# Cutting the triangle of an inversion in four pieces on two engines, and re-dealing the weight conversion steps

## The chip, the core and the metric

The kernel runs on one core of a Trainium2 chip. The metric is the device time of one execution in microseconds (us). The engines that matter are PE (TensorE, matrix products), DVE (VectorE), ACT (ScalarE), POOL (GpSimd) and SP, which here only issues DMA transfers.

## The reference, cut to what matters

A recurrent attention block feeds a two-layer network. For each of 4 batches and 8 heads a 40 x 40 state is carried over 768 time steps:

```
for t in range(S):
    y[:, :, t] = einsum('bhd,bhde->bhe', r_t, state)
    Sa = einsum('bhde,bhe->bhd', state, a_t)
    state = state * w_t[:, :, None, :] - einsum('bhd,bhe->bhde', Sa, b_t) + einsum('bhd,bhe->bhde', v_t, k_t)
x = y.transpose(0, 2, 1, 3).reshape(3072, 320)
h = x @ w_in                      # 320 x 2048
out = (h * clip(h + 3, 0, 6) / 6) @ w_out   # 2048 x 320
```

The two weight matrices are 64-bit floats in memory and are converted to 32-bit floats on the chip, once per execution.

## The kernel before, in words

Time is cut into blocks of 64 steps. Two batches and one block make a unit; there are 24 units, and four consecutive units (NU = 4) make a group, so there are six groups. Within a block the recurrence is a triangular linear system. `prepare` builds for each unit the scaled operands and the matrix F of the system (stages W, gam, A, B, F, factor, K, E, EV). `invert` then inverts, for all 32 heads of a group at once, the triangular 32 x 32 blocks of F. `third_block` joins pairs of them with matrix products, and `step` runs the recurrence of a unit (stages RT, VT, R, C, S, U, UT, rS, sn, H, y, move, move2). The two-layer network of a unit is emitted in small pieces (`expand`, `contract`) between the stages of other units, so that PE always has something to do.

`invert` runs on DVE, with one part on POOL. It transposes F into the tile `fb` (L679). POOL then copies the part below the diagonal of `fb` into the tile `x` and writes zeros elsewhere with one `affine_select` of 1024 elements in each of 128 partitions (L682), and a small memset writes ones on the diagonal (L684). Thirty steps follow, i = 1 to 30, each of one product (`prod`, L691) and one addition into `x` (L697). Step i reads column i of `x` below row i and row i left of the diagonal, and updates columns 0 to i - 1. Two more transposes give `tb` and `tt` (L700, L705), which the matrix products of `third_block` read.

The order of work is written out by hand. `invert` is a generator in the deque `side`; `aside` advances it by one product or addition. The first inversion has little other work beside it: the loop `while not third` (L1180) advances it, and after every fifth advance it runs one early stage of the first two units. The later five inversions are advanced between pieces of the network.[...]

The weight conversion is a second generator, `load_weights`. The weights come in 20 pieces. A piece needs four DVE instructions and two on ACT: a mask (L316), then two ACT instructions on `parts` (L317, L319), two DVE instructions on the raw tile (L336, L340), and after that the product that writes the converted piece (L327). The raw tiles are reused, so a new load is issued on SP (L294) as old ones come free. One step of the generator is taken wherever a table says so:

- during the first inversion, at the advances numbered in `STEPS`;
- during the steps of the first four units, after the stages listed in `PLAN`: `2C:6` means that six conversion steps are taken at each pause of stage C of unit 2. `X` and `Y` are the two `third_block` parts.

PSUM tiles of the recurrence are taken in turn from a ring of five ("any"). A product that needs a slot waits until ACT or DVE has read the slot's former content.

## Time and profile before

| What | Value |
|---|---|
| time, median of 3 runs | 813.42 us (813.09 to 814.7) |
| the profiled execution | 812.7 us, of it 811.0 us span |
| PE busy | 737.0 us (91%) |
| DVE busy | 515.8 us (64%) |
| ACT busy | 319.8 us (39%) |
| POOL busy | 175.2 us (22%) |
| mean granted TensorE clock | 0.954 |
| `fb` transpose, each of 6 | 2.15 us |
| `affine_select`, each of 6 | 1.26 us |
| diagonal memset, each of 6 | 0.16 us |

The span goes from the first to the last instruction. Times of single instructions below are counted from the span's start. "Granted clock" is the share of full speed at which the throttle let PE run in a stretch. In the timelines a number in square brackets is the time that the engine sat idle before the instruction, and the name behind the arrow is the instruction that ended the idle time; "issue" there means that the profile shows no releaser.

### The profile page before, as it was taken

How to read it: one execution, taken by the hardware profiler on the slowest of the kernel's cores; microseconds unless marked ns; L12 is line 12 of the kernel's file. 1: busy time of each engine (PE TensorE's matmuls, PEld its weight loads, DVE VectorE, ACT ScalarE, POOL GpSimd, SP SyncE). 2: the span in 40 equal slices, each digit the busy share in tenths (PEclk: the TensorE clock that was granted, in tenths of full speed). 3: DMA queues.
4: the chain of work that ended last, by engine and by line, in shares of the span. 5: the costliest groups of instructions: out<-in, count | busy, mean ns of one | idle time of the engine just before them, and what ended most of it. 6: DMA issues, size and time to landing. Idle time of an engine off the chain costs nothing.

```text
span 811.0 us, 35829 instructions
## 1 busy us (share of the span) xinstructions
PE 737.0 (91%) x15832; PEld 625.2 (77%) x15832; DVE 515.8 (64%) x1188; ACT 319.8 (39%) x846; POOL 175.2 (22%) x301
## 2 busy tenths in 40 slices
PE   4634886989999989999999999999999999999998
PEld 3623775868778868888878888878888888888886
DVE  8878878769655689555698556698345784232210
ACT  2333753231545423645334553345453324322111
POOL 6403012420222130333122223124123102000000
PEclk9955787999999999999999999999999999999999
DMA  9592653420223330332231233222222101110000
GB/s 120 108 202 54 150 158 67 75 40 18 43 52 68 56 61 11 61 66 44 40 59 32 48 66 58 41 42 44 49 50 53 19 20 30 30 21 15 17 19 16
DMA packets 174218, 45.05 MB, mean 56 GB/s; under 512 B 157424, under 2 KB 172784, under 8 KB 174064
## 3 DMA queue, kind: packets, MB, share of 16 engines
q1 hardware_dynamic: 168672, 41.87, 27.1%
q8 instruction: 125, 2.05, 1.1%
q10 hardware_dynamic: 5392, 0.90, 0.7%
q14 instruction: 29, 0.24, 0.1%
HBM read 34.08 MB, written 3.93 MB: 47 GB/s over the span
## 4 chain that ended last, share of the span: by engine, by line
PE 75%; DVE 12%; DMA 4%; issue 4%; ACT 2%; SPq 2%; POOL 1%; ACTq 0%; DVEq 0%
PE h L1009 25%; PE o L1050 23%; PE any L474 4%; PE any L436 3%; PE any L924 3%; PE any L900 2%; PE any L446 2%; PE any L805 2%; DVE x L697 2%; DVE prod L691 2%; PE any L844 1%; PE any L865 1%; DVE wm L518 1%; PE any L648 1%; DMA R<-in_r_dram 1%
## 5 line engine op out<-in xcount | busy, mean ns | idle before, releaser
L1009 PE MATMUL h<-xt,win 128*128 128x128 f32 (+1 forms) x2304 | 250.2, 282 | 8.6 <-DVE gt L1025 6.8
L1009 PEld LDWEIGHTS h<-xt,win 128*128 128x128 f32 (+1 forms) x2304 | 230.4, 191 | 26.2 <-issue 10.3
L1050 PE MATMUL o<-wout,gt 128*128 128x320 f32 x768 | 232.5, 446 | 0.0
L1050 PEld LDWEIGHTS o<-wout,gt 128*128 128x128 f32 x768 | 139.6, 192 | 51.2 <-issue 1.6
L1025 DVE SCALAR_TENSOR_TENSOR gt<-gt,h 128x512 f32<-128x512 f32 x96 | 61.9, 681 | 67.1 <-ACT gt L1024 67.0
L1024 ACT ACTIVATE gt<-h,three 128x512 f32<-128x512 f32 x96 | 62.0, 685 | 97.8 <-PE h L1009 97.6
L939 POOL TENSOR_TENSOR yg<-ys,gam 128x512 f32<-128x512 f32 x22 | 39.0, 1772 | 162.6 <-DVE ys L937 100.8
L691 DVE TENSOR_TENSOR prod<-x 128x30 f32<-128x30 f32 (+9 forms) x180 | 62.8, 349 | 12.8 <-POOL x L682 7.3
L909 DVE TENSOR_TENSOR state<-any,state 40x160 f32<-40x160 f32 (+1 forms) x88 | 27.9, 321 | 66.7 <-PE any L900 40.1
L697 DVE TENSOR_TENSOR x<-x,prod 128x30 f32<-128x30 f32 (+9 forms) x180 | 65.4, 363 | 5.4
L621 POOL TENSOR_TENSOR KBt<-K,rgt 128x320 f32<-128x320 f32 x22 | 19.0, 866 | 222.0 <-ACT rgt L611 170.0
L483 DVE COPY_PREDICATED score<-mask,any 128x256 f32<-128x256 int32 x142 | 53.0, 436 | 6.0 <-PE any L474 5.5
L937 DVE TENSOR_TENSOR ys<-any,ys 128x256 f32<-128x256 f32 x44 | 16.6, 418 | 34.6 <-PE any L648 17.9
L654 ACT ACTIVATE EV<-any 64x160 f32<-64x160 f32 x88 | 23.9, 295 | 36.3 <-PE any L648 26.7
L518 DVE TENSOR_TENSOR_SCAN wm<-wm,start 128x528 f32<-128x528 f32 x24 | 37.6, 1567 | 0.8
L784 ACT ACTIVATE RT<-any 128x256 f32<-128x256 f32 (+1 forms) x44 | 15.5, 401 | 56.6 <-PE any L446 49.8
L507 DVE TENSOR_TENSOR_SCAN prods<-wm,start 128x528 f32<-128x528 f32 x24 | 30.0, 1256 | 10.6 <-ACT wm L504 10.6
L924 PE MATMUL any<-score,KBt 64*64 64x64 f32 x1536 | 31.9, 236 | 3.5 <-DVE state L909 3.5
L924 PEld LDWEIGHTS any<-score,KBt 64*64 64x64 f32 x1536 | 28.1, 148 | 6.1 <-DVE state L909 3.6
L759 ACT ACTIVATE tinv<-any 32x256 f32<-32x256 f32 x48 | 17.9, 374 | 30.1 <-PE any L749 24.7
L528 POOL COPY gam<-prods 128x256 f32<-128x256 f32 x24 | 22.5, 937 | 30.6 <-DVE prods L507 26.7
L1068 ACT ACTIVATE ob<-o 128x320 f32<-128x320 f32 x22 | 9.5, 434 | 46.3 <-PE o L1050 25.2
(197 smaller groups left out, 1077.7 us busy)
## 6 DMA issues: line engine op xcount, KB each, us to landing
V<-in_v_dram SPq DMA_DIRECT2D x96, 40.0 KB
out_dram<-ob SPq DMA_DIRECT2D x47, 80.0 KB
R<-in_r_dram SPq DMA_DIRECT2D x92, 40.0 KB
B<-in_b_dram SPq DMA_DIRECT2D x42, 80.0 KB
K<-in_k_dram SPq DMA_DIRECT2D x42, 80.0 KB
W<-in_w_dram SPq DMA_DIRECT2D x37, 80.0 KB
A<-in_a_dram SPq DMA_DIRECT2D x37, 80.0 KB
xt<-yg SPq DMA_DIRECT2D x72, 40.0 KB
```

Source lines behind the costliest of these rows:

```text
L474: nc.tensor.matmul(out=o[i][half(q), n, :], lhsT=lhs[half(i, D), n ^ (2 * q * swap), half(q)], rhs=rhs[half(i, D), n, half(q)], start=True ...
L483: nc.vector.copy_predicated(out=x[:, 4 * i:4 * i + 4, :], mask=mask4, data=o[i])
L507: nc.vector.tensor_tensor_scan(out=prods[:].rearrange("p r m i -> p (r m i)"), data0=wm[:, 0:SCAN], data1=start[:], initial=0.0, op0=ALU.m ...
L518: nc.vector.tensor_tensor_scan(out=back, data0=back, data1=start[:], initial=0.0, op0=ALU.mult, op1=ALU.add)
L691: nc.vector.tensor_tensor(out=pv, in0=_ap(x[:], (i + 1) * L + i, [[L, n], [0, i]]), in1=_ap(x[:], i * L, [[0, n], [1, i]]), op=ALU.mult,)
L697: nc.vector.tensor_tensor(out=rest, in0=rest, in1=pv, op=ALU.add)
L924: nc.tensor.matmul(out=y[q][half(s), pr, :], lhsT=o[name][half(q), h * D:h * D + SLOT], rhs=m[name][half(q), 4 * rs + 2 * s + j, :], start ...
L939: nc.gpsimd.tensor_tensor(out=yg[:], in0=m["ys"][:].rearrange("p r q t -> p r (q t)"), in1=o["G"][:], op=ALU.mult)
L1009: nc.tensor.matmul(out=hp[c][:, i, :], lhsT=lhsT, rhs=rhs, start=(begun[c] == 0), stop=(begun[c] == 3 * NQ - 1))
L1024: nc.scalar.activation(out=gt[:], in_=hp[c][:], func=AF.Relu, bias=three[:], scale=1.0)
L1025: nc.vector.scalar_tensor_tensor(out=gt[:], in0=gt[:], scalar=6.0, in1=hp[c][:], op0=ALU.min, op1=ALU.mult)
L1050: nc.tensor.matmul(out=op[:], lhsT=gts[c][:, n, :], rhs=wout[:, c * HJ + r * NQ + n, :], start=((split or r == 0) and c == 0 and n == 0), ...
```

## The change

`x` is now made in four quarters of 16 x 16. ACT copies the lower left quarter, which lies wholly below the diagonal. POOL selects the upper left quarter and writes its diagonal, then zeros the upper right quarter, selects the lower right one and writes its diagonal. The dependence tracking gives the first product of the steps a wait for the upper left selection and for ACT's copy only; the rest of POOL's work may run beside the steps. The first wait of a step for the lower right quarter's diagonal stands at the addition of step 4.

The second and third edits deal the conversion steps by other tables. On DVE they shift the position of conversion instructions by a few places between 40 us and 140 us; on ACT they shift the `parts` pairs with them. No instruction of PE or SP changes its place.

```diff
         x = inv.tile([P, L, L], F32, name="x", tag="x", bufs=1)
-        nc.gpsimd.affine_select(out=x[:], in_=fb[:], pattern=[[1, L], [-1, L]],
-                                compare_op=ALU.is_gt, fill=0.0, base=0, channel_multiplier=0)
-        nc.gpsimd.memset(_ap(x[:], 0, [[L + 1, L]]), 1.0)
+
+        def cut(rows, columns, first):
+            nc.gpsimd.affine_select(out=x[:, rows, columns], in_=fb[:, rows, columns], pattern=[[1, HL], [-1, HL]],
+                                    compare_op=ALU.is_gt, fill=0.0, base=0, channel_multiplier=0)
+            nc.gpsimd.memset(_ap(x[:], first * (L + 1), [[L + 1, HL]]), 1.0)
+
+        HL = L // 2
+        nc.scalar.activation(out=x[:, HL:, 0:HL], in_=fb[:, HL:, 0:HL], func=AF.Copy)
+        cut(slice(0, HL), slice(0, HL), 0)
+        nc.gpsimd.memset(x[:, 0:HL, HL:], 0.0)
+        cut(slice(HL, L), slice(HL, L), HL)
         for _ in range(3):
             yield
...
-    STEPS = (1, 6, 8, 9, 10, 14, 17, 25, 31, 36, 42, 48, 58, 61, 64)
+    STEPS = (2, 4, 9, 12, 13, 16, 20, 24, 26, 31, 39, 52, 59, 61, 64)
...
-    PLAN = """X X:2 0U:3 0UT 1R
-              0sn 0H:2 Y:2
-              1U:1 1UT:3 0y:4
-              2RT:2 Y
-              1sn 1H 2VT:2 0move 0move2
+    PLAN = """X:1 X:1 0U:3 0UT 1R
+              0sn:1 0H:2 Y:2
+              1U 1UT:3 0y:2
+              2RT:1 Y
+              1sn:1 1H:1 2VT:1 0move 0move2
               1y:3 2R
-              2S:3 3RT
-              1move 1move2 2U:1 2UT 2C:6
-              3R:3 3VT
+              2S:3 3RT:1
+              1move 1move2 2U:1 2UT 2C:7
+              3R:3 3VT:1
               2rS:3 2sn:3 2H:4 3S:2
-              2y:2 3U:3 3UT:7 3C:5
-              3rS:4 3sn 3H 2move
-              3y 2move2
+              2y:3 3U:2 3UT:7 3C:5
+              3rS:2 3sn:1 3H:2 2move
+              3y:2 2move2
```

## The prediction

> **What bounds the kernel now.** I read the page first (busy shares, granted clock), then the groups of the inversion's lines, then the table by stretches, then the timelines of DVE, POOL, ACT, PE and SP where PE stops.

> ```profile
> PE 737.0 (91%) x15832; PEld 625.2 (77%) x15832; DVE 515.8 (64%) x1188; ACT 319.8 (39%) x846; POOL 175.2 (22%) x301
> PE   4634886989999989999999999999999999999998
> PEclk9955787999999999999999999999999999999999
> ```

> PE is the bound. From about 140 us on it hardly stops; before that it waits for DVE, DMA and ACT. As its order and work stay, time is gained only where PE stands still or runs at a lower clock. Now the inversion:

> ```profile
> L682 POOL TENSOR_SCALAR_AFFINE_SELECT x<-fb x6: 1264/1264/1267, 29.3 to 633.5; 128x1024 f32<-128x1024 f32 x6
>   DVE prod L691: 7.3, 6
> ```

> DVE waits 7.3 us in all for POOL's selection: 0.39 us in the first group, 1.37 to 1.43 us in the other five. Whether that costs anything is told by the stretches (PE, PEld, DVE, ACT, POOL busy; clock; DMA) and, below the dots, by the timeline (start, duration, engine).

> ```profile
> 174.00:176.00 2.00, 1.98 (x43) 1.24 (x36) 1.10 (x3) 0.00 (x0) 1.94 (x5) 1.00 0.00 0
> 176.00:178.00 2.00, 0.00 (x0) 0.00 (x0) 1.93 (x3) 0.00 (x0) 2.00 (x4) 1.00 0.00 0
> 178.00:180.00 2.00, 0.81 (x24) 0.84 (x28) 1.83 (x7) 0.00 (x0) 0.35 (x1) 0.86 0.66 112
> 180.00:185.00 5.00, 5.00 (x69) 3.62 (x62) 3.63 (x12) 2.17 (x8) 0.00 (x0) 0.72 0.18 34
> ...
> 174.83 0.20 DVE L691 TENSOR_TENSOR prod<-x 128x30 f32<-128x30 f32 x1 [1.43 <-POOL x L682]
> 175.07 0.86 DVE L697 TENSOR_TENSOR x<-x,prod 128x30 f32<-128x30 f32 x1
> 178.66 0.76 DVE L483 COPY_PREDICATED score<-mask,any 128x256 f32<-128x256 int32 x2
> 174.99 0.87 POOL L621 TENSOR_TENSOR KBt<-K,rgt 128x320 f32<-128x320 f32 x1
> 179.19 1.36 PE L648 MATMUL any<-V,score 64*64 64x40 f32 x32 [3.21 <-issue]
> ```

> In the second inversion PE stands from 175.98 to 179.19. The profile names no releaser, but the product L648 reads the masked score, which DVE writes from 178.66 behind three step pairs: the inversion's late start is PE's wait. After it the clock falls: 1 us windows show 0.50 from 180 to 182, and the four L1050 products there take 2.43 us against 1.27.

> ```profile
> 394.18 2.15 DVE L679 STREAM_TRANSPOSE fb<-F 128x1024 f32<-128x1024 f32 x1 [4.65 <-ACT F L591]
> 397.71 0.21 DVE L691 TENSOR_TENSOR prod<-x 128x30 f32<-128x30 f32 x1 [1.37 <-POOL x L682]
> 415.17 1.13 PE L1009 MATMUL h<-xt,win 128*128 128x128 f32 x8 [1.26 <-DVE gt L1025]
> ```

> In the fourth inversion DVE has no further idle time from 397.71 to the gt at 414.42 for which PE waits 1.26 us. The fifth is a copy of it (PE waits 1.26 us at 531.94); the third waits 1.43 us at 293.00, again for gt. After the sixth (from 631.30) no PE wait is listed.

> ```profile
> 41.26 0.43 DVE L316 TENSOR_SCALAR parts<-tinv 128x512 uint32<-128x512 uint32 x1 [1.08 <-DMA tinv<-in_moe_w_in_dram]
> 58.29 0.78 DVE L483 COPY_PREDICATED score<-mask,any 128x256 f32<-128x256 int32 x2 [2.78 <-PE any L474]
> ```

> In the first inversion DVE waits at 41.26 for a weight load and at 58.29, by way of PE, for the load of R. What is won before these is waited away.

> **The new gate.** DVE's first product waits for the later of two. POOL's selection of 256 elements: by the row of 1024 (1.264 us), 0.32 us if time goes with elements, 1.26 if none of it does; POOL copies of 256 elements took 0.40, so I take 0.43. ACT's copy of 256 elements: the ACT copy of 320 elements within SBUF (L799) took 0.46, those of 256 from PSUM 0.37 to 0.40; I take 0.43. ACT was idle at the end of fb in inversions two to five, so the gate falls from 1.26 to 0.43: DVE starts 0.83 us earlier. POOL's five pieces sum to 0.43 + 0.15 + 0.30 (memset of 256, between rows of 0.25 for 192 and 0.16 for 32) + 0.43 + 0.15 = 1.46 us against 1.26 + 0.16: KBt, queued behind them, moves by 0.1 us.

> [...] The rows: the addition at 175.07 took 0.86 us beside POOL's KBt product, and 0.21 us in the fourth inversion without it, while the product at 30.59 took 0.20 us beside POOL's diagonal memset. [...] The second selection reads `fb` and now stands beside the steps; before, DVE idled through it. [...] I take 0.3. On ACT the copy waits for fb with all behind it: rgt (second inversion, to 174.6, needed at 175.1), RT (third, 0.4 us late, read only behind network pieces), gt (sixth: 631.29 becomes 633.9, but DVE takes it at 634.7 instead of 635.46).

> **The sum, against the profiled 812.7 us.**

> *27 to 72 us.* DVE's stream starts 0.39 us earlier and meets both waits above. `STEPS` puts the same 12 conversion instructions before the last transpose, and the same three behind the score of 58.29, so `tb` stays at 67.84. 0 us (0.5 better to 1 worse).

> *72 to 140 us.* At 76 to 80 DVE idles 3.52 us; `PLAN` moves one L340 (0.60) into it. The next parts pair on ACT ends 0.6 us earlier, so does zs behind it, for which PE's L865 waits 0.47 us at 83.56. PE's L749 then ends 0.4 us earlier than 88.23, which frees tile x for the load at 88.33. From there SP issues back to back until 116.58, and the last but two of its weight loads (115.45, landed 120.85) starts the DVE chain of conversions, score, scans and gt that ends with the state at 136.26, for which PE waits 3.51 us. That chain keeps its sum (L327, 0.6, moves from its end to its middle). So -0.4 us. ACT's S at 98.74 comes some 1.5 us earlier, but U now stands behind another pair and ends where it did: nothing.
> One step turns the other way: U of unit 3 (ACT, 117.99) now stands behind the parts pair of the load of 120.85, so at 122.8. The score product L474, which needs U's ring slot, moves from 118.05 to 123.1, and what follows it at half clock (1.2 + 0.95 + 1.1 + 0.95 + 1.0 us) ends L436 at 128.2 instead of 126.04. PE had 3.5 us to spare before 136.54, so this costs nothing, and leaves a shorter stop ahead of 136 us. After the stop the clock is at 0.50 until about 141.9, 2.7 us of PE work lost. I count 1.0 of these as saved. Together -1.4 us (from 1 worse to 3.1 better).

> *Second inversion.* fb ends at 173.41, the gate at 173.96; two pairs are through by 175.0, the third pair meets KBt (two of its instructions cost one POOL product each, 0.85), the score starts at 176.9 and PE at 177.4: 1.8 us less (1.0 if a fourth instruction is caught, 2.6 if only one). PE's stop is then 1.4 us. Does the clock fall? Rows: stops of 3.21, 2.89 and 2.61 us (from 176, 110.6 and 96.8) were each followed by some 3.4 us at 0.50, the stop of 1.43 us at 291.6 by none. [...] I go by the trace: 3.4 us x 0.5 = 1.7 us saved. Together -3.5 us (1.0 to 4.3).

> *Third to fifth.* DVE's chain to the gt shortens by 0.83 - 0.3 = 0.53 us, less than PE's waits of 1.43, 1.26 and 1.26: -1.6 us (0.9 to 2.5). What is late next is the same gt, by 0.7 us. *Sixth.* 0.

> Sum -6.5: 806.2 for an execution like the profiled one. That lay 0.7 below the median of 813.42, so the median goes to 806.9.

> **The rivals.**
> *Clock not saved (0.27).* The stop stays over 2 us, or the clock falls anyway; 72 to 140 gives 0.4. For it: the shortest stop seen before a fall is 2.61 us, so the limit may be just above 1.43. 0.4 + 1.8 + 1.6 = 3.8 less: 809.6.
> *The wait changes its name (0.10).* The selection is mostly fixed cost, or ACT's copy waits behind F and wakes late: the first product starts as before and the collision with the second selection eats the rest. For it: nothing shows a selection of 256. Against: POOL's times grow with elements (memsets: 0.16 for 32, 1.80 for 2048). 813.0.
> *Slower (0.08).* U of unit 3 behind the conversion pair, at 118 to 128 us. Each us that the load lands later holds U, the score, and both transposes of W; past PE's slack (3.5 less 2.1 used) it counts fully, and it decides the sign once it exceeds all else, when the load lands over 6 us after 120.85. Against: SP's order is unchanged, and this load took 5.4 us, the longest other 6.35. Then 816.

> **How the numbers follow.** The forecast has 0.55: 806.9, own range 804 to 809. The measurement can tell about 0.2%, 1.6 us. Faster (under 811.8) are the forecast, the first rival and 0.02 of the second: 0.84. Same 0.08 (the rest of the second), slower 0.08. The range, 803.9 to 812.0, takes in the better bounds of all terms in part and the first rival whole.

> **What would show it.** Right: the first product 0.5 us after fb instead of 1.3; PE's stop at 176 under 2 us and no 0.50 in the clock behind it; the waits for gt in inversions three to five near 0.7 us; `tb` of the first still some 9.5 us behind the score. Wrong: a selection of 256 near 1 us; steps of 0.6 us beside the second selection; PE stopped past 137 us for a score or transpose queued behind U.

## The result, and the profile after

The changed kernel took 808.35 us (median of 4 runs, 807.46 to 809.5) where the kernel before took 813.25 us beside it (4 runs, 812.76 to 814.7). The ratio is 0.9938, with a 95% interval of 0.9917 to 0.9958: 5 us or 0.6% faster. Measured again, they stood at 807.88 (12 runs) and 812.35 us (26 runs), ratio 0.995 (0.9931 to 0.9968). The forecast was 806.9.

The profiled execution took 807.46 us, of it 805.7 us span. Lines of the page that answer to those shown of before (busy time, then the span in 40 slices):

```profile
PE 737.2 (91%) x15832; PEld 625.7 (78%) x15832; DVE 516.3 (64%) x1188; ACT 322.5 (40%) x852; POOL 177.2 (22%) x319
PE   4734868999999989999999999999999999999998
PEclk7755788999999999999999999999999999999999
```

PE does the same work, 737 us, in a span that is 5.3 us shorter; ACT has six instructions more, POOL eighteen. The time was gained where PE stood still. The new pieces, by tile (min, median and max in ns), and who waited for the selection:

```profile
L684 POOL TENSOR_SCALAR_AFFINE_SELECT x<-fb x12: 505/506/508, 29.4 to 629.4; 128x256 f32<-128x256 f32 x12
L686 POOL MEMSET x<- x12: 126/128/130, 30.0 to 629.9; 128x16 f32 x12
L691 POOL MEMSET x<- x6: 312/312/313, 30.2 to 629.1; 128x256 f32 x6
L689 ACT ACTIVATE x<-fb x6: 416/417/417, 29.3 to 628.3; 128x256 f32<-128x256 f32 x6
  DVE prod L699: 3.1, 5
```

DVE waits 3.1 us for the selection in place of 7.3. The line numbers have moved: L684 is the selection (L682 before), L699 the product (L691), L705 the addition (L697), and what follows `invert` stands 8 lines lower. The second inversion, from the timeline (start, duration, engine, operation, in brackets the idle time before it):

```profile
169.85 0.51 POOL L684 TENSOR_SCALAR_AFFINE_SELECT x<-fb 128x256 f32<-128x256 f32 x1 [14.79 <-issue]
170.39 0.21 DVE L699 TENSOR_TENSOR prod<-x 128x30 f32<-128x30 f32 x1 [0.67 <-POOL x L684]
...
170.87 0.51 POOL L684 TENSOR_SCALAR_AFFINE_SELECT x<-fb 128x256 f32<-128x256 f32 x1
170.87 0.53 DVE L699 TENSOR_TENSOR prod<-x 128x58 f32<-128x58 f32 x1
...
171.56 0.86 POOL L621 TENSOR_TENSOR KBt<-K,rgt 128x320 f32<-128x320 f32 x1
...
171.70 0.82 DVE L699 TENSOR_TENSOR prod<-x 128x84 f32<-128x84 f32 x1
172.38 0.86 POOL L621 TENSOR_TENSOR KBt<-B,rgt 128x320 f32<-128x320 f32 x1
172.56 0.78 DVE L705 TENSOR_TENSOR x<-x,prod 128x84 f32<-128x84 f32 x1
...
173.26 0.76 DVE L483 COPY_PREDICATED score<-mask,any 128x256 f32<-128x256 int32 x2
...
173.79 0.89 PE L648 MATMUL any<-V,score 64*64 64x40 f32 x30 [1.49 <-issue]
```

Three things are to be seen. The gate, DVE's wait for the selection, is 0.67 us, 1.43 before. The second selection more than doubles the second product: 0.53 us, where the fourth inversion of before, with nothing on POOL beside it, has 0.22:

```profile
398.19 0.22 DVE L691 TENSOR_TENSOR prod<-x 128x58 f32<-128x58 f32 x1
```

And of the three step pairs ahead of the score only two instructions meet KBt and are long now (0.82, 0.78), where four had been (0.86, 0.79, 0.83, 0.81), as POOL starts KBt one and a half step pairs later in DVE's count. PE's stop falls from 3.21 to 1.49 us. The table of the stretches cut at 3.40 us (length; busy PE, PEld, DVE, ACT, POOL; granted clock; DMA share; GB/s) shows what follows:

```profile
171.40:174.80 3.40, 1.91 (x67) 1.54 (x66) 3.19 (x8) 0.03 (x1) 3.37 (x7) 0.99 0.02 2
174.80:178.20 3.40, 3.40 (x37) 2.07 (x37) 3.08 (x10) 1.06 (x4) 0.16 (x1) 0.51 0.59 99
```

The clock falls to half for 3.4 us all the same. In the fourth inversion the wait for gt goes from 1.26 to 0.83 us:

```profile
391.11 0.21 DVE L699 TENSOR_TENSOR prod<-x 128x30 f32<-128x30 f32 x1 [0.62 <-POOL x L684]
...
391.60 0.53 DVE L699 TENSOR_TENSOR prod<-x 128x58 f32<-128x58 f32 x1
...
408.89 1.13 PE L1017 MATMUL h<-xt,win 128*128 128x128 f32 x8 [0.83 <-DVE gt L1033]
```

Ahead of it, between the first and the second transpose:

```profile
56.75 0.77 DVE L483 COPY_PREDICATED score<-mask,any 128x256 f32<-128x256 int32 x2 [2.62 <-PE any L474]
117.41 0.43 DVE L316 TENSOR_SCALAR parts<-raw_fb 128x512 uint32<-128x512 uint32 x1 [0.99 <-DMA raw_fb<-in_moe_w_out_dram]
119.59 1.13 PE L474 MATMUL any<-RT,VT 40*64 40x64 f32 x30 [3.36 <-ACT U L857]
133.62 1.89 PE L932 MATMUL any<-score,KBt 64*64 64x64 f32 x62 [2.85 <-DVE state L917]
```

The score in the first of these lines (58.29 before) is called the first score below. All of them stand 1.5 to 3.4 us earlier than before, except L474, which waits 3.36 us for U behind the conversion pair and still ends with 2.85 us to spare.

Where the 5.3 us of the two spans lie is read from the six transposes `fb`, which start each inversion. From one to the next the two profiled executions took, before and after: 144.29 and 140.47; 110.86 and 108.73; 112.09 and 112.06; 116.78 and 117.62; 120.34 and 120.15 us. So -3.8 between the first and the second, -2.1 in the second, and in sum +0.6 over the third to fifth, where -1.6 had been forecast.

### The profile page after: what moved, and what is told of

It reads as the page before. It is cut to its first block, busy times and chain, and to the rows that moved or that the text cites. A ratio compares the mean times of both kernels' runs of the same rounds, so it can differ in the third digit from the quotient of the medians.

```text
span 805.7 us, 35863 instructions
## 1 busy us (share of the span) xinstructions
PE 737.2 (91%) x15832; PEld 625.7 (78%) x15832; DVE 516.3 (64%) x1188; ACT 322.5 (40%) x852; POOL 177.2 (22%) x319
## 3 DMA queue, kind: packets, MB, share of 16 engines
q8 instruction: 125, 2.05, 1.0%
## 4 chain that ended last, share of the span: by engine, by line
PE 72%; DVE 10%; issue 5%; DMA 4%; ACT 2%; SPq 1%; POOL 1%; ACTq 0%; DVEq 0%; POOLq 0%
PE h L1017 25%; PE o L1058 23%; PE any L474 4%; PE any L436 3%; PE any L932 3%; PE any L446 2%; PE any L908 2%; DVE prod L699 2%; PE any L813 2%; DVE x L705 2%; PE any L852 1%; DMA R<-in_r_dram 1%; PE any L648 1%; PE any L873 1%; PE any L757 1%
## 5 line engine op out<-in xcount | busy, mean ns | idle before, releaser
L699 DVE TENSOR_TENSOR prod<-x 128x30 f32<-128x30 f32 (+9 forms) x180 | 64.3, 357 | 8.6 <-POOL x L684 3.1
L705 DVE TENSOR_TENSOR x<-x,prod 128x30 f32<-128x30 f32 (+9 forms) x180 | 65.2, 362 | 5.4
L621 POOL TENSOR_TENSOR KBt<-K,rgt 128x320 f32<-128x320 f32 x22 | 19.1, 866 | 217.7 <-ACT rgt L611 214.1
L483 DVE COPY_PREDICATED score<-mask,any 128x256 f32<-128x256 int32 x142 | 53.0, 436 | 6.0 <-PE any L474 5.6
L528 POOL COPY gam<-prods 128x256 f32<-128x256 f32 x24 | 22.5, 938 | 29.9 <-DVE prods L507 26.0
```

What stands on the lines that cost most here:

```text
L483: nc.vector.copy_predicated(out=x[:, 4 * i:4 * i + 4, :], mask=mask4, data=o[i])
L699: nc.vector.tensor_tensor(out=pv, in0=_ap(x[:], (i + 1) * L + i, [[L, n], [0, i]]), in1=_ap(x[:], i * L, [[0, n], [1, i]]), op=ALU.mult,)
L705: nc.vector.tensor_tensor(out=rest, in0=rest, in1=pv, op=ALU.add)
```

## The experiments

My theory after the result: the gate (0.67 us for 1.43) and the DVE steps that are long beside POOL's products (two of about 0.8 us for four) make the second inversion's gain, the tables make that ahead of it, and the rest of the differences belongs to single executions. The rivals: the early first score is the change's own, the collision eats the gate, or the gain comes from one of the edits alone.

**The selection in quarters alone.** `invert` of the changed kernel, `STEPS` and `PLAN` of before.

```diff
-    STEPS = (2, 4, 9, 12, 13, 16, 20, 24, 26, 31, 39, 52, 59, 61, 64)
+    STEPS = (1, 6, 8, 9, 10, 14, 17, 25, 31, 36, 42, 48, 58, 61, 64)
...
-    PLAN = """X:1 X:1 0U:3 0UT 1R
+    PLAN = """X X:2 0U:3 0UT 1R
...
```

> The selection in quarters alone, with STEPS and PLAN as before. My theory (the inversion's gate and the tables gain in different places): inversions 2 to 5 as in the changed kernel (PE's stop ahead of the EV products in the second one 1.5 us in place of 3.2, waits for gt near 0.8 in place of 1.26), so the second inversion brings 2.1 us and the later ones little more; what the changed kernel had won before its second transpose (3.67 us) mostly stays away, because it hangs on the order of the tables. About 810.5 us, 2.2 faster than the kernel before. Rival A (the early 1.5 us at the first score belong to the earlier start of the steps): the score near 58.3 us comes at 56.8 here too, and the time is about 809. Rival B (the collision of the second selection with the second product, 0.31 us in each inversion, and KBt on GpSimd beside the third step eat the gate's gain): no change, 812.5 to 813.5.

809.25 us, ratio to before 0.9965 (0.9947 to 0.9984), some 3 us. First score at 57.34 (rival A had 56.8; before has 58.29), the second transpose at 170.90, and from there 108.85 us to the third. PE's waits in that stretch (us in total, times, longest):

```profile
PE any L648 <- issue: 1.5, 1, 1.5
```

The gate works alone as it does with the tables; rival B, no change, falls.

**The tables alone.**

```diff
+        nc.gpsimd.affine_select(out=x[:], in_=fb[:], pattern=[[1, L], [-1, L]],
+                                compare_op=ALU.is_gt, fill=0.0, base=0, channel_multiplier=0)
+        nc.gpsimd.memset(_ap(x[:], 0, [[L + 1, L]]), 1.0)
-        def cut(rows, columns, first):
...
```

> STEPS and PLAN of the changed kernel with the whole triangle selected by GpSimd as before. My theory: the stretch between the third blocks and the second inversion gains about 2 us (raw_x load about 0.3 earlier, raw_fb converted about 3 us earlier), the first score stays near 58 us or moves to 57, the second transpose comes 2 to 3.5 us sooner, and from there on every wait is that of before (PE's stop 3.2 us, waits for gt 1.26 to 1.43): 809.5 to 811. Rival A (the early 1.5 us belong to the earlier start of the steps): the second transpose comes only 2.1 us sooner, about 811. Rival B (the tables only fit the new steps' timing): no gain or a loss, 813 to 815.

810.95 us, ratio 0.9987 (0.9968 to 1.0006): about 1 us less, which the measurement cannot tell from nothing. First score at 55.71, earlier than expected and the earliest of all profiles, second transpose at 167.56 us, raw_fb converted at 118.28, then the waits of before:

```profile
PE any L648 <- issue: 3.2, 2, 3.1
```

**Both kernels once more, unchanged.**

> The changed kernel as it is, for a second profile. If what was won by the first score (58.3 to 56.8 us) and in the landing of raw_fb (5.4 to 4.4 us after its issue) belongs to the change, both stand here as before: score near 56.8, raw_fb converted near 117.4 us, time 807.5. If they belong to one execution only, the score comes between 57 and 58.5 or raw_fb a microsecond later, and the time is about 809.4, the other of the two values that the four runs took. PE's stop in the second inversion 1.5 us and the half clock after it for one or two windows of 3.4 us: in my theory the fall is a matter of how the stop lies to the windows and may be absent in this profile.

> The kernel before as it is, for a second profile. If the 1.5 us at the first score and the 1 us of raw_fb's landing are the change's: score at 58.3 us, R issued at 40.4 and raw_fb converted at 120.8 us again. If they vary from one execution to the next: one of them 1 us or more off. The clock after the three long stops of PE (2.6, 2.9 and 3.2 us) falls to half again.

| profile of | first score | raw_x load | raw_fb converted | second `fb` | third `fb` |
|---|---|---|---|---|---|
| before | 58.29 | 88.33 | 120.85 | 171.23 | 282.09 |
| before, again | 57.13 | 87.43 | 120.58 | 170.98 | 281.41 |
| after | 56.75 | 86.52 | 117.41 | 167.56 | 276.29 |
| after, again | 56.35 | 86.26 | 118.95 | 170.04 | 277.67 |

The repeat of before has its first score at 57.13 and its R issued at 39.57 in place of 40.37: with nothing changed it moves by 1.2 us. The repeat of after stays early, at 56.35. Of the 3.7 us by which the second transpose came early, 2.5 are gone in the repeat of after, although its raw_x load is as early. The second inversion's stop is 1.47 us again, and this time the clock does not fall (1.00 behind the stop), as my theory allowed: the stretch takes 107.63 us in place of 108.73.

**One table each.** PLAN of the changed kernel with the old `STEPS`, then `STEPS` with the old `PLAN`, quarters in both.

> The changed kernel with the STEPS table of before: quarters and PLAN only. My theory (the score of the first window comes between 56 and 58.4 us from one execution to the next, whatever STEPS says; PLAN's earlier third-block pieces bring raw_x, the conversion of raw_fb and so the second transpose forward): from the first score to the raw_x load 29.0 to 29.9 us as in the changed kernel (30.0 to 30.3 before), the second transpose near 169.5 us, 808.5 in all. Rival (STEPS brings it, by the order of the conversion pieces among the first steps): raw_x 30.1 us behind the score, second transpose near 171, 809.5 in all.

> The changed kernel with the PLAN of before: quarters and STEPS only. My theory: raw_x load 30.0 to 30.3 us behind the first score, second transpose near 171 us as in both profiles of the kernel before and with the quarters alone, 809.5 in all. Rival (STEPS brings the gain): second transpose near 169.5 us, 808.5.

808.33 us, ratio 0.9954 (0.9937 to 0.997), and 809.78 us, ratio 0.9967 (0.9949 to 0.9986): by time they can't be told apart. By the profiles, from the first score to the raw_x load 29.07 us with the new `PLAN` alone and 30.02 with the old, as my theory had it. The second transpose stands at 169.80 and 170.06, the latter between the two expectations. Over all profiles the stretch between the first and second transpose took 143.14 to 144.29 us in the four with the old `PLAN` (mean 143.8) and 140.47 to 143.53 in the ten with the new one (mean 142.3), those of the experiments below with them.

**KBt off GpSimd.** In the second group's last two units the two KBt products of each go to VectorE, behind the scores.

```diff
...
+            if NU + 2 <= i < 2 * NU:
+                o["late"] = rest
+            else:
+                rest(nc.gpsimd)
...
+            if "late" in o:
+                o.pop("late")(nc.vector)
...
```

Here `rest` holds the two products, and the second part stands in the stage EV, behind the scores.

> The changed kernel, with the four KBt products of the second group's last two units taken from GpSimd and given to VectorE behind the scores. My theory (while GpSimd multiplies two tensors, VectorE's steps stand still: 0.82, 0.78 and 0.75 us where such a step takes 0.22 to 0.27 alone): the third step's pair takes 0.5 us in place of 1.60, PE's stop ahead of the EV products falls from 1.49 to 0.4 us, and as the 3.41 us window with the stop is then busy to over 0.8, the clock doesn't fall after it. VectorE pays four products of 0.5 us and gets back about 1.6. In all 1.1 to 2 us less than the changed kernel, 806.5 where that one has 808. Rival (the long pairs are long for their own reasons, or the next wait ends just as late): the stop stays near 1.4 us, and the time is 808 to 809, by the added work on VectorE.

807.01 us, ratio 0.9931 (0.991 to 0.9951). From its timeline:

```profile
173.15 0.53 DVE L707 TENSOR_TENSOR prod<-x 128x58 f32<-128x58 f32 x1
...
173.96 0.25 DVE L707 TENSOR_TENSOR prod<-x 128x84 f32<-128x84 f32 x1
174.24 0.25 DVE L713 TENSOR_TENSOR x<-x,prod 128x84 f32<-128x84 f32 x1
174.41 0.76 DVE L483 COPY_PREDICATED score<-mask,any 128x256 f32<-128x256 int32 x2
...
174.94 0.40 PE L654 MATMUL any<-V,score 64*64 64x40 f32 x4 [0.35 <-issue]
```

The third pair takes 0.50 us in place of 1.60 and PE's stop goes to 0.35: that KBt on POOL held the steps up is shown. The clock holds (1.00 from 174.7 to 181.5 us). But the stretch takes 107.64 us, as in the repeat of after, whose clock also held: the 1.1 us of stop were given back. Two new waits of PE, 0.17 for the state and 0.26 for zs, stand near the third blocks, which need the end of the inversion, and that end came hardly sooner (tb 30.43 us behind the transpose, 30.56 in the repeat). The rival on the next wait holds for this part, and by time this run can't be told from the changed kernel.

**The second selection only written.** The lower right quarter is filled with zeros in place of being selected; its data are left out.

```diff
-        cut(slice(HL, L), slice(HL, L), HL)
+        nc.gpsimd.memset(x[:, HL:, HL:], 0.0)
+        nc.gpsimd.memset(_ap(x[:], HL * (L + 1), [[L + 1, HL]]), 1.0)
```

> The changed kernel with the second selection, that of the lower right quarter, replaced by a fill with zeros of the same 256 elements: that quarter's data are left out. My theory (an instruction of GpSimd that reads SBUF keeps the two-input product of VectorE waiting, one that only writes does not): the second product takes 0.22 us in place of 0.53 in each of the six inversions, PE's waits for gt in the third to fifth fall from 0.8 to 0.5 us. About 1 us less than the changed kernel in all, 0.3 in the profile at each. Rival (the product is slow because two engines write the same tile, or by its shape): 0.53 us stays and nothing moves.

```profile
172.34 0.31 POOL L692 MEMSET x<- 128x256 f32 x1
172.37 0.22 DVE L700 TENSOR_TENSOR prod<-x 128x58 f32<-128x58 f32 x1
...
PE h L1018 <- DVE gt L1034: 0.5, 1, 0.5
```

Same tile, same elements, but POOL only writes: the product is back at 0.22 us, and the wait for gt in the fourth inversion at 0.51 in place of 0.83. So the product is longer by 0.31 us beside a selection that reads `fb`, and not beside a fill that only writes, and the 0.31 us pass to PE in full (0.32). 807.63 us, ratio 0.9934 (0.9907 to 0.996); 1 us is too little for the time to show.

**The transpose in halves.** The first half brings the columns that the first selection and ACT's copy read, so these run beside the second half.

```diff
+        for part in (slice(0, L // 2), slice(L // 2, L)):
+            nc.vector.transpose(out=fb[:, :, part].rearrange("p t s -> p s t"),
+                                in_=F[:, :, part].rearrange("p h s -> p s h"))
-        nc.vector.transpose(out=fb[:].rearrange("p t s -> p s t"),
-                            in_=F[:, :, 0:L].rearrange("p h s -> p s h"))
```

> The changed kernel with the transpose ahead of the inversion in two halves, so that the first selection and ScalarE's copy run beside the second half. My theory (the gate is a bare wait, and a transpose with one input does not exclude GpSimd): VectorE's wait of 0.67 us for the first selection goes to 0.0 to 0.1 in inversions 2 to 6; the halves cost 0.05 to 0.1 us more together; the second selection now collides with the first step in place of the second, for 0.3 to 0.5 us. Net 0.3 to 0.6 us for each of inversions 2 to 5: PE's waits for gt 0.8 to about 0.4, the stop in the second inversion 1.49 to about 1.0 and no fall of the clock after it. 806 where the changed kernel has 808. Rival (the selection does collide with the transpose, or the step loses what the gate won): no change, 808.

```profile
170.02 2.22 DVE L680 STREAM_TRANSPOSE fb<-F 128x512 f32<-128x512 f32 x2 [0.39 <-ACT F L572]
...
171.33 0.50 POOL L685 TENSOR_SCALAR_AFFINE_SELECT x<-fb 128x256 f32<-128x256 f32 x1 [13.81 <-PE any L606]
...
172.13 0.17 DVE L700 TENSOR_TENSOR prod<-x 128x30 f32<-128x30 f32 x1
...
172.57 0.35 DVE L700 TENSOR_TENSOR prod<-x 128x58 f32<-128x58 f32 x1
...
175.31 0.54 PE L648 MATMUL any<-V,score 64*64 64x40 f32 x6 [0.30 <-issue]
```

804.73 us, ratio 0.9902 (0.9882 to 0.9921): 7.8 us below before, the lowest median of all. The first step has no wait, the first selection takes its 0.50 us beside the transpose, the second adds only 0.13 us to the second product (0.35), and PE's stop, expected at 1.0, is 0.30. PE's wait for gt in the fourth and fifth inversion is 0.26 us. In the third it stays at 0.93 (0.98), because the gate stays there:

```profile
278.29 0.87 POOL L621 TENSOR_TENSOR KBt<-B,rgt 128x320 f32<-128x320 f32 x1
279.12 0.50 POOL L685 TENSOR_SCALAR_AFFINE_SELECT x<-fb 128x256 f32<-128x256 f32 x1
279.66 0.21 DVE L700 TENSOR_TENSOR prod<-x 128x30 f32<-128x30 f32 x1 [0.50 <-POOL x L685]
```

The first half is there at 278.09, but POOL is busy with KBt until 279.1, when the second half ends too.

**KBt on VectorE and the transpose in halves together.**

> Both of the last: the transpose in halves, and the four KBt products on VectorE behind the scores. My theory: the two add up. PE's stop in the second inversion is gone (under 0.3 us), the clock holds, waits for gt in the later inversions 0.4 us: 805 to 805.5, the fastest of all. Rival: PE's next wait (for R, for gt) takes the place of the stop, and the time stays at 806.5 or above.

806.25 us, ratio 0.9911 (0.9889 to 0.9933). PE's stop is gone, yet the stretch takes 106.90 us against 106.88 with the halves alone. The two do not add up; the rival stands. By time it can't be told from the halves alone.

**V loaded later.** This asked for the stops at the score product L474 in the third to fifth inversion.

```diff
-            if i > 2 * NU:
-                fetch("V", i)
             for name in "BK":
...
             o["E"] = masked(x)
+            if i > 2 * NU:
+                fetch("V", i)
```

> The changed kernel with the load of V in the later groups (units past 2 NU) issued behind the scores' masking in place of behind KBt. It asks where the gain of the waits for gt in the third to fifth inversion went: in every profile PE stands still for 0 to 1.3 us at one score product some 64 to 71 us behind each transpose, about 1.9 us after the first V load's issue, with no wait that the profile shows. My theory (the V loads' traffic holds PE's own supply up): with V later these stops go from PE's list at that product, and come elsewhere at most in part; 1 to 2 us less than the changed kernel. Rival (the stop belongs to the place in PE's program, or to its own completion counts): it stays at that product, 0.6 to 1.3 us in two or three of the three groups, and the time is unchanged at 808.

> The same move of the V load on the kernel with the transpose in halves, the fastest so far. My theory: 803.5 to 804.5, the stops at the score product gone, waits for gt 0.26 in the fourth and fifth inversion. Rival: 804.7 as with the halves alone, the stops still there; or V comes late for its EV product and PE waits for it, 806.

822.39 us, ratio 1.0129 (1.0101 to 1.0156), and 822.48 us, ratio 1.0123 (1.0092 to 1.0154). My theory failed in both; that V comes late was a rival of the second, at 806. Between the second and the third transpose PE now waits for V itself:

```profile
PE any L648 <- DMA V<-in_v_dram: 10.8, 5, 6.4
```

The clock was at half in five windows of that stretch, four besides. The stops at L474 stayed (1.00 and 0.92 us in the third and fourth inversion, none in the fifth): the V load issued just ahead of that product is not one of those that the edit moved, so the question was not put.

## Why the prediction was right, and where it was not

The direction was right, and 808.35 us lies within the range of 804 to 809. But the first rival, in which the clock is not saved, had 809.6: the measured time lies between the two, 1.4 us from the forecast and 1.3 from the rival. By the forecast's own steps:

- *The new gate.* Selection of 256: 0.51 us, taken as 0.43. ACT's copy: 0.42, taken as 0.43. The gate fell by 0.76 us, not 0.83. That a selection is mostly fixed cost, the second rival, could have been ruled out before: the profile of before has three small selections while the kernel sets up, and those of 64 elements took 0.24, the one of 128 took 0.29 us, against 1.26 for 1024.
- *The second selection beside the steps.* Right, in sign and size: 0.31 us in each inversion from the second (0.53 us for 0.22), 0.3 taken. The 0.3 was the author's estimate: before has no selection beside a step, only KBt products, and no run made ahead of the forecast shows the term. In its place the runs showed the second product at 0.53 us beside the selection, which reads, and at 0.22 us beside the fill, which only writes.
- *27 to 72 us, nothing.* Probably wrong by about 1 us. Of the profiles with the whole transpose, the first score came at 55.7 to 57.7 us in the seven with the new `STEPS` (mean 56.5) and at 57.1 to 58.3 in the four with the old (57.7). R was issued at 38.8 and 39.9 us on the mean. With scatter of over 1 us in either group this is not proof, and how `STEPS` would do it stays open.
- *72 to 140 us, -1.4.* Right on the mean of the profiles: from the first score to the second transpose 113.5 us in the four with the old `PLAN`, 112.2 in the ten with the new. The raw_x load came 0.7 us earlier behind the score (0.4 forecast). Behind PE's stop before 137 us the clock was at half for two windows of 3.41 us in three of the four, and for one or none in all ten. That U of unit 3 would go behind the conversion pair at no cost was right (wait 3.36 us, 2.85 us left). By time alone the tables' gain isn't shown.
- *Second inversion, -3.5.* The restart was right: the masked score starts 5.70 us behind the start of `fb`, forecast 5.67, and PE's stop is shorter by 1.72 us, forecast 1.8. The clock term, 1.7, failed. In six profiles the kernel is that of after up to this stop, but for the tables (after, its repeat, the quarters alone, one table each, V later). The stop was 1.47 to 1.49 us in all, and the clock fell in five. The stretch took 108.55 us on the mean of the first five, 110.65 on that of the two profiles of before: 2.1 us less. The step that failed is "I go by the trace": a stop's length was read as the criterion, with that of 1.43 us at 291.6 as the case without a fall. Falls come in windows of 3.41 us on one grid in each profile, and that stop lay across the edge of two, at 292.07 (PE busy for 0.85 of the one and 0.73 of the other, the clock at 1.00 behind both). How the stop lies to the windows is what the runs show in its place. Whole inside one, it left PE busy for 0.56 to 0.57 of it, and the clock fell, five times of five. In the repeat of after 0.18 us of it lay in the window before:

```profile
174.90:178.30 3.40, 2.04 (x36) 1.53 (x36) 3.23 (x9) 1.04 (x4) 2.53 (x4) 1.00 0.24 42
178.30:181.70 3.40, 3.40 (x55) 3.23 (x55) 3.16 (x11) 1.13 (x5) 0.00 (x0) 1.00 0.46 84
```

These cuts lie within 0.07 us of the windows. On the windows themselves PE was busy for 0.62 here and for 0.56 in the profile after, whose clock fell. Even a fall avoided was worth less than 1.7 us: the stretch took 107.63 us without it, in this one profile, and 108.64 to 108.91 with it.

- *Third to fifth, -1.6.* The waits for gt fell by 0.43 to 0.47 us each (forecast 0.53), some 1.35 in all, in the first five of these profiles. Yet the three stretches took 348.8 us on their mean, and 348.9 in the two profiles of before (351.2 with the tables alone, of it 1.7 for a fall of the clock). What the sum had not foreseen are PE's stops at L474: 2.5 us on the mean of the five (1.6 to 3.5), 1.9 and 1.3 in the two of before. They cover 0.9 of the missing 1.2 us; the rest stays open.

In the two profiles that were forecast and compared, luck made up for this: 3.8 us were won ahead of the second transpose where 1.4 had been forecast, of which 2.6 were gone in the repeat. That stood in for two thirds of the 3.6 us missing in the second inversion and behind it. The changed kernel's own gain, over all runs, is 4 to 5 us, between the forecast's sum of 6.5 and the first rival's 3.8, and nearer to the rival.

## What to carry to other kernels

Where VectorE and GpSimd work side by side, ask not only when an instruction can start but what the neighbour does while it runs: here a product took 0.53 us beside a selection that reads and 0.22 us beside a fill, and over half of what the restart in the second inversion gained (0.96 of 1.72 us) came from GpSimd products that met two VectorE steps in place of four. A bare wait can also go by cutting the instruction ahead of it, so that its first half releases the next engine: here 0.67 us to none in the second inversion. Before a stretch is credited to a change, profile both kernels a second time: stretches of 140 us moved by 2.6 us with nothing changed.

## What the runs showed of the hardware

**The stops at L474 go with late instruction packets.** They come amid a series of equal products, and the profile names no releaser. The queues' part lists one queue as instruction; its packets hold 16 KB (125 of them, 2.05 MB, in either profile). Around the fourth inversion's L474, in the profile after (456.5 to 459.5 us, with the stop, PE going on at 459.01) and before (460 to 464, none; the product at 464.08):

```profile
q8 instruction: 1, 0.02, 2.6%
...
q8 instruction: 1, 0.02, 2.2%
```

One packet each. After, it starts at 456.5 us, 6.2 us behind the last one, and PE goes on 2.5 us later. Before, it starts at 461.1, 4.5 us behind the last one, and PE does not stop. So it is in the third to fifth inversion of all 14 profiles, 42 stretches. In the 33 with a stop the packet starts 4.6 to 6.8 us behind the last one, and PE goes on 2.2 to 2.9 us after it. In the nine without, it starts 3.6 to 4.5 us behind the last one, and the product 3.0 to 3.2 us after it. No run moved such a packet, so that it is the cause is argued and not shown; why it comes late stays open.
